# Sparse attention and mixture of experts: early pieces with the weights as fixed operand, and 232 rows for the last two ranks

## The chip, the core and the metric

The kernel runs on one core of a Trainium2 chip. A core has TensorE (PE, whose weight loads the profile lists apart as PEld), VectorE (DVE), ScalarE (ACT), GpSimd (POOL) and SyncE (SP), which work side by side and wait for each other on semaphores. The metric is the device time of one execution in microseconds (us). Before the change the median of three runs is 350.05 us (350.0 to 353.05).

## The reference, cut to what matters

```python
scores = scale * np.matmul(q, k.transpose(0, 1, 3, 2))      # 4 batches, 8 heads, 576 positions, 64 wide
scores = np.where(masks, scores, -1e9)                      # 4 heads: a window of 32; 4 heads: every 32nd position
attn = softmax(scores); x = (attn @ v) as 2304 tokens x 512
logits = x @ w_gate                                         # 8 experts
expert_idx = argmax(logits); gate_w = softmax(logits)[expert_idx]
h = maximum(x_of_expert @ w1[e], 0)                         # 512 -> 1024
y = h @ w2[e]                                               # 1024 -> 512
out[token] = gate_w * y                                     # all float32; an expert takes at most 576 tokens
```

With the inputs of the reference's seed the eight experts get 348, 339, 329, 279, 278, 271, 231 and 229 tokens.

## The kernel before, in words

**Attention and routing** come first. PE, DVE and ACT walk through an order written out by hand. As logits become known, the tokens get an expert and a place in its list (`r_top`, `r_pos`, `r_slot`, `r_tab`: short DVE chains with small matmuls between them, all in the PSUM tile `R_`).

**The expert that will be the fullest is known early**, from the first 1536 tokens. While the routing of the last tokens still runs, its first 128 tokens ("the pieces") go through the whole expert in plain float32. This is the generator `early` (L932 to L971). `up(c)`, for c of 0 to 3, makes 128 tokens x 256 features: the turned tokens `x` are the fixed operand (lhsT), the weights `loads[c][0]` the moving one, 256 columns wide, over four slices of the 512 inputs. ACT takes the maximum with 0 (L946, tile `hs`). Features then have to lie on partitions for the second layer, so `turn(c)` (L949) turns two 128 x 128 blocks on PE with the identity (L952), and ACT copies them to `ht` (L953). `down(f)` (L955), for f of 0 to 7, adds one slice of the second layer to `y0p`, 128 x 512; ACT copies the sum to `keep["y"]` (L971). `ep(k)` runs k steps of the generator, and L1035 to L1094 place these steps among the routing's last matmuls. In float32 each matmul instruction of the program shows as two matmuls and two weight loads in the profile, called passes below; a turn shows as one. `x_steps(1)` and `x_steps(2)` (L1067 to L1077, matmuls L1072) turn the next two gathered blocks of tokens of this expert, for the stage after.

**The expert stage** takes the experts by rank of their token count. How many rows each rank has is fixed by a tuple of `SETS`; the smallest set that holds all counts is chosen by a branch (L1447). Rank 0 has 352 - 128 = 224 rows left, since the pieces took 128. Numbers are split in two halves of type fp32r, so each product is three matmuls. `gemm1` (L1254) is 12 matmuls for each of 8 blocks of features, with the weights fixed and the tokens moving, n columns wide. Where n is at most 256 (`tm`: rank 0 and the last two ranks), the second layer is `gemm2_t` (L1277): 6 matmuls per block, whose moving operand is the weights, always 512 wide. The other ranks use `gemm2`, n wide. Weights stream in ahead of use.

**PSUM** has eight banks. Before the expert stage: `ps_t` three banks, `ps_s` one tile of two (banks 3 and 4), `ps_o` one tile of two (5 and 6), `R_` one. `h0` and `y0p` are both tiles of `ps_s`, `h1` is of `ps_o`. In the expert stage `ps_y` has the banks 0 to 3, `ps_h` the banks 4 and 5 (the first `ph` is in bank 4), `ps_x` the banks 6 and 7. A tile of the new stage waits for the last reader of the old tile in the same bank.

Of the kernel before, what the change touches and what calls it, by code (L numbers as in the profile page):

```python
# [9 lines left out]
F32 = mybir.dt.float32  # L10
# [4 lines left out]
AF = mybir.ActivationFunctionType  # L15
# [17 lines left out]
WARM = 9  # L33
SPLIT = (3, 4, 5)
SETS = (
# [3 lines left out]
)  # L39
# [12 lines left out]
def kernel(  # L52
# [10 lines left out]
    nc = tc.nc  # L63
# [6 lines left out]
    KD = DM // 128  # L70
# [28 lines left out]
    ident = const.tile([128, 128], F32, name="ident")  # L99
# [51 lines left out]
    with ExitStack() as p1:  # L151
# [5 lines left out]
        wk = p1.enter_context(tc.tile_pool(name="wk", bufs=3))  # L157
        tmp = p1.enter_context(tc.tile_pool(name="tmp", bufs=2))
        ps_t = p1.enter_context(tc.tile_pool(name="ps_t", bufs=3, space=PSUM))
        ps_s = p1.enter_context(tc.tile_pool(name="ps_s", bufs=1, space=PSUM))  # L160
# [753 lines left out]
        regs, loads, g0 = {}, {}, {}  # L914
# [17 lines left out]
        def early(x):  # L932

            h = [ps_s.tile([128, 2, 512], F32, tag="s", name="h0"), None]
            hs = wk.tile([128, 4, 2, 128], F32, tag="x", name="hs0", bufs=2)
            ht = wk.tile([128, 8, 128], F32, tag="x", name="ht0", bufs=2)
            y = None

            def up(c):
                if c == 1:  # L940
                    h[1] = ps_o.tile([128, 2, 512], F32, tag="o", name="h1")
                o = h[c % 2][:, c // 2, 0:256]
                for d in range(KD):
                    nc.tensor.matmul(o, lhsT=x[:, d], rhs=loads[c][0][:, d], start=d == 0, stop=d == KD - 1)
                    if d == KD - 1:
                        nc.scalar.activation(hs[:, c].rearrange("p a f -> p (a f)"), o, AF.Relu)  # L946
                    yield

            def turn(c):  # L949
                t = ps_t.tile([128, 2, 128], F32, tag="t", name="th0")  # L950
                for a in range(2):
                    nc.tensor.transpose(t[:, a], hs[:, c, a], ident)  # L952
                nc.scalar.copy(ht[:, 2 * c:2 * c + 2], t)  # L953

            def down(f):  # L955
                nc.tensor.matmul(y, lhsT=ht[:, f], rhs=loads[f // 2][1][:, f % 2], start=f == 0, stop=f == NF - 1)
                yield

            for c in range(4):
                u = up(c)  # L960
                next(u)
                yield
                if c:
                    turn(c - 1)
                yield from u
            y = ps_s.tile([128, 2, 512], F32, tag="s", name="y0p")[:, 0]
            for f in range(NF):
                if f == 1:
                    turn(3)
                yield from down(f)  # L970
            nc.scalar.copy(keep["y"], y)  # L971

# [4 lines left out]
        for i in range(-1, n):  # L977
# [11 lines left out]
            if i == n - 1:  # L989
                work0 = early(early_x())  # L990
# [491 lines left out]
```

## Time and profile before

| | us |
|---|---|
| median of three runs | 350.05 |
| the profiled execution | 347.72 |
| its span, first to last instruction | 346.0 |
| attention and routing, up to the first matmul of the pieces | 0 to 104.6 |
| pieces, beside the routing's last tokens | 104.6 to 124.3 |
| eight experts on PE | 125.0 to 340.7 |
| last scaling, last scatter to memory | 340.7 to 346.0 |

A profile lists for each engine when it was busy and what ended its idle time. An idle time matters only on an engine that others wait for, or that is itself never free later.

### The profile page before, as it was taken

What the parts mean: (1) busy time and instruction counts of PE and PEld (TensorE: products, weight loads), DVE (VectorE), ACT (ScalarE), POOL (GpSimd) and SP (SyncE); (2) the same over time, 40 slices, a digit from 0 to 9 for tenths busy, and PEclk for the clock granted to TensorE, in tenths of its full rate; (3) what the DMA queues carried; (4) which work ended last, traced back from release to release, by engine and by line L of the source; (5) the groups of instructions that cost most, each with busy time, mean ns of one, the idle gap of its engine ahead of it and who ended that gap; (6) DMA issues with size and microseconds to landing.
All of it is one profiled execution on the core that took longest, in us unless ns stands there. A gap on an engine that the chain in (4) does not pass through costs nothing. (4 is left out here: it accounts for less than half of the span.)

```text
span 346.0 us, 9916 instructions
## 1 busy us (share of the span) xinstructions
PE 333.6 (96%) x4023; PEld 295.6 (85%) x4024; DVE 213.3 (62%) x480; ACT 181.8 (53%) x342; POOL 119.9 (35%) x154
## 2 busy tenths in 40 slices
PE   8998999999999999999999999999999999999993
PEld 4777778777677568899999999999999999989992
DVE  7546466778975846654556555765765666665650
ACT  7686868767453344654434345354444454455531
POOL 8459456435010233065321450252251151121402
PEclk9999999999999999999999999999999999999998
DMA  6998998626099258078545554765575565665201
GB/s 207 310 216 269 277 185 241 150 73 132 20 311 350 61 181 265 19 214 276 191 136 159 176 184 122 234 219 176 170 252 145 193 224 189 192 231 147 101 1 64
DMA packets 51796, 62.85 MB, mean 182 GB/s; under 512 B 13622, under 2 KB 37192, under 8 KB 51741
## 3 DMA queue, kind: packets, MB, share of 16 engines
q1 hardware_dynamic: 47773, 52.20, 51.5%
q0 software_dynamic: 3968, 9.93, 8.3%
q8 instruction: 33, 0.54, 0.7%
q14 instruction: 22, 0.18, 0.2%
HBM read 52.67 MB, written 9.60 MB: 180 GB/s over the span
## 5 line engine op out<-in xcount | busy, mean ns | idle before, releaser
L1250 PE MATMUL ph<-xh,w1h 128*128 128x280 f32 (+5 forms) x252 | 76.8, 305 | 0.0
L1252 PE MATMUL ph<-xh,w1l 128*128 128x280 f32 (+5 forms) x252 | 74.0, 294 | 0.0
L1251 PE MATMUL ph<-xl,w1h 128*128 128x280 f32 (+5 forms) x252 | 74.0, 294 | 0.0
L1267 ACT ACTIVATE hh<-ph 128x280 fp32r<-128x280 f32 (+5 forms) x64 | 25.9, 405 | 89.3 <-PE ph L1252 87.1
L1295 POOL DMA_INDIRECT out_dram<-yo,routing x22 | 21.8, 992 | 122.2 <-DVE yo L1328 83.1
L1268 DVE SCALAR_TENSOR_TENSOR hl<-ph,hh 128x280 fp32r<-128x280 f32 (+5 forms) x64 | 28.8, 450 | 54.0 <-ACT hh L1267 54.0
L1250 PE MATMUL y<-hh,w2h 128*128 128x280 f32 (+3 forms) x160 | 48.2, 301 | 0.0
L1250 PEld LDWEIGHTS ph<-xh,w1h 128*128 128x128 f32 x252 | 47.6, 189 | 0.7
L1251 PE MATMUL y<-hl,w2h 128*128 128x280 f32 (+3 forms) x160 | 48.2, 301 | 0.0
L1252 PE MATMUL y<-hh,w2l 128*128 128x280 f32 (+3 forms) x160 | 48.2, 301 | 0.0
L1251 PEld LDWEIGHTS ph<-xl,w1h 128*128 128x128 f32 x252 | 47.7, 189 | 0.5
L1252 PEld LDWEIGHTS ph<-xh,w1l 128*128 128x128 f32 x252 | 47.6, 189 | 0.0
L1230 DVE TENSOR_TENSOR w1l<-w1r,w1h 128x1024 fp32r<-128x1024 f32 x31 | 38.0, 1226 | 15.0 <-ACT w1h L1229 13.9
L1230 DVE TENSOR_TENSOR w2l<-w2r,w2h 128x1024 fp32r<-128x1024 f32 x31 | 38.0, 1225 | 11.6 <-ACT w2h L1229 11.1
L1229 ACT CAST w2h<-w2r 128x1024 fp32r<-128x1024 f32 x31 | 32.2, 1040 | 0.0
L1229 ACT CAST w1h<-w1r 128x1024 fp32r<-128x1024 f32 x31 | 32.2, 1040 | 0.0
L1252 PEld LDWEIGHTS y<-hh,w2l 128*128 128x128 f32 x160 | 30.1, 188 | 0.0
L1250 PEld LDWEIGHTS y<-hh,w2h 128*128 128x128 f32 x160 | 30.1, 188 | 0.0
L1251 PEld LDWEIGHTS y<-hl,w2h 128*128 128x128 f32 x160 | 30.1, 188 | 0.0
L1340 POOL DMA_INDIRECT gt<-g_dram,routing x22 | 24.8, 1127 | 13.5 <-DMA xg<-x_dram,idx 7.1
L142 POOL DMA_INDIRECT xg<-x_dram,routing x19 | 19.3, 1014 | 24.0 <-PE px L1240 13.5
L224 POOL COPY v0l<-v0l 32x1088 f32<-32x1088 f32 x16 | 18.3, 1141 | 7.8 <-DMA v0l<-in_v_dram 6.9
(237 smaller groups left out, 629.8 us busy)
## 6 DMA issues: line engine op xcount, KB each, us to landing
w1r<-in_moe_w_dram SPq DMA_DIRECT2D x32, 512.0 KB
w2r<-in_moe_w_dram SPq DMA_DIRECT2D x32, 512.0 KB
vz<-in_v_dram SPq DMA_DIRECT2D x16, 144.0 KB
lk<-in_k_dram SPq DMA_DIRECT2D x4, 576.0 KB
lq<-in_q_dram SPq DMA_DIRECT2D x4, 576.0 KB
v0l<-in_v_dram SPq DMA_DIRECT2D x16, 144.0 KB
x_dram<-xz SPq DMA_DIRECT2D x16, 144.0 KB
x_dram<-xl SPq DMA_DIRECT2D x8, 256.0 KB
```

Of the source, the lines that this page charges most:

```text
L142: nc.gpsimd.indirect_dma_start(out=t[:r], out_offset=None, in_=x_dram[0:rows, :], in_offset=bass.IndirectOffsetOnAxis(ap=idx[:r], axis=0),)
L224: nc.gpsimd.tensor_copy(vt[64 * h:64 * h + 32, 1:18, h, 0:64], vt[64 * h + 32:64 * h + 64, 0:17, h, 0:64])
L1229: nc.scalar.copy(hi, t)
L1230: nc.vector.tensor_tensor(lo, t, hi.bitcast(F32), op=ALU.subtract)
L1250: nc.tensor.matmul(o, lhsT=wh, rhs=xh, start=first, stop=False)
L1251: nc.tensor.matmul(o, lhsT=wh, rhs=xl, start=False, stop=False)
L1252: nc.tensor.matmul(o, lhsT=wl, rhs=xh, start=False, stop=last)
L1267: nc.scalar.activation(hh, o, AF.Relu)
L1268: nc.vector.scalar_tensor_tensor(hl, o, 0.0, hh.bitcast(F32), op0=ALU.max, op1=ALU.subtract)
L1295: s = nc.gpsimd.indirect_dma_start(out=out[:, :], out_offset=bass.IndirectOffsetOnAxis(ap=idx, axis=0), in_=o, in_offset=None, bounds_chec ...
L1340: nc.gpsimd.indirect_dma_start(out=t[:r], out_offset=None, in_=g_dram[:, :], in_offset=bass.IndirectOffsetOnAxis(ap=idx_r(i)(j)[:r], axis=0),)
```

## The change

Three things change. In `up(c)` the weights become the fixed operand and the 128 turned tokens the moving one: the result lies with its features on partitions, ACT writes the maximum with 0 straight into `ht`, and `turn`, `hs` and ACT's copies go. Each of the 16 matmuls of 256 columns becomes two of 128; the generator yields as often as before. `y0p` moves from the two banks of `ps_s` to one bank of `ps_t`. The last two ranks of the smallest set get 232 rows instead of 256. Lines behind this place stand 9 lower in the new program (L1261 is L1252 there, L1447 is L1438).

```diff
-    (352, 344, 336, 280, 280, 272, 256, 256),
+    (352, 344, 336, 280, 280, 272, 232, 232),
...
-            hs = wk.tile([128, 4, 2, 128], F32, tag="x", name="hs0", bufs=2)
             ht = wk.tile([128, 8, 128], F32, tag="x", name="ht0", bufs=2)
...
                 o = h[c % 2][:, c // 2, 0:256]
-                for d in range(KD):
-                    nc.tensor.matmul(o, lhsT=x[:, d], rhs=loads[c][0][:, d], start=d == 0, stop=d == KD - 1)
-                    if d == KD - 1:
-                        nc.scalar.activation(hs[:, c].rearrange("p a f -> p (a f)"), o, AF.Relu)
-                    yield
-
-            def turn(c):
-                t = ps_t.tile([128, 2, 128], F32, tag="t", name="th0")
                 for a in range(2):
-                    nc.tensor.transpose(t[:, a], hs[:, c, a], ident)
-                nc.scalar.copy(ht[:, 2 * c:2 * c + 2], t)
+                    for d in range(KD):
+                        nc.tensor.matmul(
+                            o[:, 128 * a:128 * a + 128], lhsT=loads[c][0][:, d, 128 * a:128 * a + 128], rhs=x[:, d],
+                            start=d == 0, stop=d == KD - 1,
+                        )
+                        if a and d == KD - 1:
+                            nc.scalar.activation(ht[:, 2 * c:2 * c + 2].rearrange("p a f -> p (a f)"), o, AF.Relu)
+                        if d % 2:
+                            yield
...
             for c in range(4):
-                u = up(c)
-                next(u)
-                yield
-                if c:
-                    turn(c - 1)
-                yield from u
-            y = ps_s.tile([128, 2, 512], F32, tag="s", name="y0p")[:, 0]
+                yield from up(c)
+            y = ps_t.tile([128, 512], F32, tag="t", name="y0p")
             for f in range(NF):
-                if f == 1:
-                    turn(3)
                 yield from down(f)
             nc.scalar.copy(keep["y"], y)
```

On PE, between the tables of the tokens before last (`R_` at L672) and the positions of the last ones (L628), the second and third `up` and one turn (`th`) stood among the routing; h are the sums of `up`:

```order
-L944 MATMUL h_2558<-w1r,x_2462 128x256 x2
-L944 MATMUL h_2511<-w1r,x_2462 128x256
-L952 MATMUL th_2610<-ident,hs_2512 128x128 x2
-L944 MATMUL h_2511<-w1r,x_2462 128x256
+L944 MATMUL h_2561<-x_2462,w1r 128x128 x4
+L944 MATMUL h_2511<-x_2462,w1r 128x128 x4
 L628 LDWEIGHTS tri
 L628 MATMUL R__129<-oh,tri 128x16
```

Four matmuls of 256 columns and two turns became eight matmuls of 128 columns, ahead of the same L628.

On ACT, from the first sum of the pieces to their last:

```order
-L946 ACTIVATE hs_2512<-h_2511 128x256
-L1041 CAST w1h<-w1r 128x1024
-L545 COPY xtl<-txl 128x512
-L953 COPY ht_2513<-th_2560 128x256
-L946 ACTIVATE hs_2512<-h_2558 128x256
-L953 COPY ht_2513<-th_2610 128x256
+L949 ACTIVATE ht_2512<-h_2511 128x256
+L1032 CAST w1h<-w1r 128x1024
+L545 COPY xtl<-txl 128x512
+L949 ACTIVATE ht_2512<-h_2561 128x256
```

The copies of the turned blocks are gone; the cast of the first expert's weights (`w1h`) and the copy `xtl` stay behind the first maximum.

On PE at the start of the expert stage, with the engines whose semaphores are waited for; before:

```order
L956 MATMUL y0p<-w2r,ht_2513 128x512 [waits DMAHW4_49,Activation_49]
L956 MATMUL y0p<-w2r,ht_2513 128x512
L1447 COMPARE_AND_BRANCH
L1261 MATMUL ph<-xh,w1h 128x224 [waits Activation_49]
L1261 MATMUL ph<-xh,w1h 128x224 x3
```

and now:

```order
L954 MATMUL y0p<-w2r,ht_2512 128x512 [waits DMAHW4_49,Activation_49]
L954 MATMUL y0p<-w2r,ht_2512 128x512
L1438 COMPARE_AND_BRANCH
L1252 MATMUL ph<-xh,w1h 128x224 [waits PE_49,Activation_49]
L1252 MATMUL ph<-xh,w1h 128x224 x3
```

Before, the first `ph` waited for ACT's copy of `y0p` (L971). Now it waits for ACT's cast of the last turned tokens, the instruction ahead of that copy, and for PE matmuls of `up`, long ahead.

## Rows read from the trace of the kernel before

**Rows 1.** The page: busy time, and the clock granted to TensorE in 40 slices.

```profile
PE 333.6 (96%) x4023; PEld 295.6 (85%) x4024; DVE 213.3 (62%) x480; ACT 181.8 (53%) x342; POOL 119.9 (35%) x154
...
PEclk9999999999999999999999999999999999999998
```

**Rows 2.** All waits of PE from 104 us on: total us, times, longest.

```profile
PE ph L1261 <- ACT y L971: 0.8, 1, 0.8
PE LPl L576 <- ACT xtl L545: 0.4, 1, 0.4
PE R__129 L672 <- DVE r_pe L637: 0.3, 1, 0.3
```

**Rows 3.** Timeline of PE, pieces' stage: start, duration, line, tiles [idle before].

```profile
107.88 0.38 PE L952 MATMUL th<-ident,hs 128*128 128x128 f32 x2
...
109.07 0.31 PE L576 MATMUL LPl<-wg,xtl 128*32 128x8 f32 x16 [0.36 <-ACT xtl L545]
...
109.91 1.54 PE L944 MATMUL h<-w1r,x 128*128 128x256 f32 x6
...
112.21 0.17 PE L628 MATMUL R__129<-oh,tri 128*128 128x16 bf16 x1
...
112.79 1.54 PE L944 MATMUL h<-w1r,x 128*128 128x256 f32 x6
...
115.08 0.26 PE L672 MATMUL R__129<-r_rh,r_ol 128*128 128x40 bf16 x4
115.19 1.11 PE L944 MATMUL h<-w1r,x 128*128 128x256 f32 x4
116.13 1.02 PE L956 MATMUL y0p<-w2r,ht 128*128 128x512 f32 x2
116.99 0.38 PE L952 MATMUL th<-ident,hs 128*128 128x128 f32 x2
117.21 1.88 PE L956 MATMUL y0p<-w2r,ht 128*128 128x512 f32 x4
...
121.52 2.74 PE L956 MATMUL y0p<-w2r,ht 128*128 128x512 f32 x6
125.03 0.68 PE L1261 MATMUL ph<-xh,w1h 128*128 128x224 f32 x4 [0.77 <-ACT y L971]
```

**Rows 4.** Timeline of ACT, the same stage.

```profile
108.43 0.59 ACT L545 COPY xtl<-txl 128x512 f32<-128x512 f32 x1
...
124.30 0.59 ACT L971 COPY y<-y0p 128x512 f32<-128x512 f32 x1 [1.99 <-PE y0p L956]
```

**Rows 5.** Timeline of DVE: the last tokens' table operands.

```profile
114.03 0.32 DVE L657 TENSOR_TENSOR r_rh<-r_oa,vali 128x160 bf16<-128x160 bf16 x1
```

**Rows 6.** Timeline of POOL: the second gather of tokens ahead of the experts.

```profile
116.03 1.13 POOL L142 DMA_INDIRECT xg<-x_dram,idx  x1 [1.38 <-DVE t L730]
```

**Rows 7.** DMA issues from 100 to 130 us: these gathers, median us to landing.

```profile
xg<-x_dram,idx POOLq DMA_INDIRECT x2, 3.5
```

**Rows 8.** PE timeline: 12 first-layer matmuls, rank 0 (224 columns), then rank 7 (256).

```profile
132.01 0.27 PE L1250 MATMUL ph<-xh,w1h 128*128 128x224 f32 x1
...
133.34 0.40 PE L1282 MATMUL y<-w2h,hh 128*128 128x512 f32 x1
...
327.86 0.28 PE L1250 MATMUL ph<-xh,w1h 128*128 128x256 f32 x1
...
329.28 0.39 PE L1282 MATMUL y<-w2h,hh 128*128 128x512 f32 x1
```

**Rows 9.** Groups by line and shape: busy us, mean ns of one.

```profile
L1250 PE MATMUL ph<-xh,w1h 128*128 128x256 f32 x64 | 18.5, 289 | 0.0
...
L1250 PE MATMUL ph<-xh,w1h 128*128 128x344 f32 x32 | 10.5, 328 | 0.0
...
L944 PEld LDWEIGHTS h<-w1r,x 128*128 128x128 f32 x32 | 5.3, 190 | 0.3
```

**Rows 10.** Instructions of the branch on PE's queue: shortest, median, longest ns; first and last start.

```profile
L1447 PEldq COMPARE_BRANCH  x2: 90/1810/3529, 120.1 to 336.5; - x2
```

**Rows 11.** Timeline of the weight loads at the start of the experts.

```profile
125.00 0.52 PEld L1261 LDWEIGHTS ph<-xh,w1h 128*128 128x128 f32 x4 [1.56 <-issue]
```

**Rows 12.** Timeline of POOL: the last scatter.

```profile
341.71 1.02 POOL L1295 DMA_INDIRECT out_dram<-yo,routing  x1 [1.77 <-POOLq L1447]
```

## The prediction, made before the run

> **What bounds the kernel now.** I read the page first: PE is busy 96% of the span, and its clock is granted in full throughout [rows 1], so a change counts where it shortens PE's own chain. Busy shares are averages, so the next view is the list of everything that PE waited for after 104 us: three waits, 1.5 us in all [rows 2]. From the first expert matmul at 125.03 us to the end of its work PE waits for nothing: whatever PE saves there, and any earlier start of that stage, comes off the end. Then the timeline of PE in the pieces' stage [rows 3], where each start is read against the one before.
>
> **The weights as fixed operand.** A pass of 256 columns costs 0.215 us: six of them last 1.54 us and four 1.11 [rows 3], 0.43 for two more. A pass of 512 costs 0.43 (2.74 less 1.88 for two more). So 128 columns stream in about 0.107 us, and the 32 passes become 64 with the same columns in all. What is new is a weight load per 128 columns. The trace has no float32 pass of 128 columns with fresh weights. The nearest row is the first layer of rank 0: each matmul of 224 columns brings its own 128 x 128 load, and 12 take 133.34 - 132.01 = 1.33 us, 0.111 each [rows 8]. The load is of the same kind there (the pieces' own is listed with 190 ns [rows 9]; the cadence shows that most of this lies under the matmul before). Bounds for the pass: 0.107, the columns alone, and 0.218, columns and load one after the other (0.107 + 0.111). I take 0.111, because the row at 0.111 has the same load and nearly as many nanoseconds of columns.
>
> Now along PE. The first 16 passes end where eight did, within 0.05 us. The turn at 107.88 goes for nothing: PE then waits for ACT's `xtl` until 109.07, and this copy stands on ACT behind the first maximum and the weight cast, which do not move [rows 3, 4]. From 109.91: before, six passes, a turn and two passes reach L628 at 112.21, 2.30 us. After, 16 passes need 16 x 0.111 = 1.78, plus 0.08 for the first pass of a run, whose load nothing hides (four passes from 115.19 take 0.94 until 116.13, not 0.86 [rows 3]): 1.86. **Gain 0.44.** That turn cost twice its own time because PE waited for ACT in front of it. The next run is alike, from 112.79 to L672 at 115.08: 2.29 becomes 1.86, gain 0.43, in all 0.87. L672 also needs DVE's operands, ready at 114.35 before [rows 5] and, as their chain hangs on L628, 0.44 earlier now, at 113.91; PE arrives at 114.21, so PE is still the later one, by 0.3 us. Four passes (0.94) become eight (0.97), gain 0.84. The turn at 116.99 goes: 117.21 - 116.99 = 0.22, in all **1.06 us**. What could be late next is the gather for the second turned block: issued at 116.03, landed 3.5 us later at 119.5 [rows 6, 7]. Its index comes from the table that L672 closes, so it moves 0.87 earlier, to 118.7, and PE wants it at about 120. No wait.
>
> ACT loses four copies, which nobody on the path waited for; `hs` frees SBUF only: nothing.
>
> **The sums in one bank.** `y0p` ends its six passes at 121.52 + 6 x 0.43 = 124.10, its copy on ACT runs from 124.30 to 124.89 [rows 4], and the first expert matmul, whose bank was that of `y0p`, starts at 125.03: 0.93 us in which PE issues nothing. Now this matmul waits for ACT's cast of the last turned tokens, which in the new times is done about 2 us before. So it can follow the last pass at once, at 124.10 - 1.06 = 123.04: **gain 1.99 us with the above**. The banks that `y0p` takes now belong to the second layer, first written over 2 us later, when the copy is done. Hidden under the old wait is the branch: PE's queue held its compare up to 3.53 us, from 120.1 to 123.6 [rows 10], then the first new weight load came at 125.00 [rows 11], just after the copy. How much of the 1.4 us between is the branch's own cannot be seen; ends are 0 and all of it. I take 0: the compare ends just as the last pass issues, and that pass lasts 0.43 us, cover for a restart of that size. If this cover is too short it is a rival below.
>
> **232 rows.** Twelve matmuls of 256 columns take 329.28 - 327.86 = 1.42 us, 0.118 each, against 0.111 for 224 [rows 8]. At 224 the weight load sets the pace, not the columns (0.093 at the full clock); 232 columns with the 0.012 that 256 show above their columns come to 0.108, still below the load. So 0.111, and 2 ranks x 96 x 0.0075 = **1.44 us**. Bounds: 1.1 if the pace is read off a straight line between 224 and 256, 1.9 if columns alone counted (24 columns, 10 ns each, 192 times). The second layer moves 512 columns per matmul whatever the rows: nothing. ACT's and DVE's tiles shrink by a tenth, off the path. The last scatter takes 1.02 us for 128 rows [rows 12], is on the path, and has 104 now: 0 to 0.2, I take 0.1.
>
> Here a rule of the Trainium skill differs: TensorE: Matmul & The Clock Gate, section Back-to-back issue gap, gives the isolated gap as columns / 2.4 plus 2.5 ns, so by this estimate 109 ns for 256 and 99 for 232. By it the two ranks would save 1.9 us and the whole change 4.0. The trace has 118 and, for 224 columns, 111 [rows 8]; it decides.
>
> **Sum.** 1.99 + 1.44 + 0.1 = 3.5 us. The profiled execution of 347.72 us would take 344.2. The runs' median is 350.05, 2.3 above the profiled one; the same saving from it gives **346.5 us**.
>
> **The rivals.**
> *The weight loads do not hide* (ends slower). If a float32 pass cannot run beside the load of the next, it costs 0.218 instead of 0.111. The 16 passes ahead of the first maximum delay ACT's cast and `xtl`, and so L576, by 16 x 0.107 = 1.7 us; 40 passes after it add 4.3. Together 6.0 us against the forecast: 352.5, 0.7% slower than before. It decides from a pass of about 0.17 us on, where 56 passes eat the 3.5. Against it: the cadence of 0.111 in rank 0 [rows 8], less than load and columns in sequence could give. For it: no row has just this form, and the float32 load is listed with 190 ns [rows 9]. Chance 6%.
> In the same page of the Trainium skill, section The mechanism says that a weight load overlaps running matmuls only where it goes to another row group; all loads here use every row. By that rule this rival would be the forecast; the trace contradicts it at 224 columns.
> *The branch takes the place of the wait.* If all of the 1.4 us after the compare is the branch's own, the expert stage starts at 125.03 - 1.06 = 123.97, the gain is 2.6 and the time 347.5. For it: nothing is seen between 123.6 and 125.00 [rows 11]. Against it: the wait for the copy explains that gap alone, to 0.1 us. Chance 14%.
> *The narrow ranks give nothing*: another limit in the last two ranks (weights arriving, ACT, DVE) takes over. The time is 350.05 - 2.1 = 348. Against it: rank 0 runs at 224 columns with the same work beside it and PE waits for nobody [rows 2]. Chance 6%.
> *The smallest set no longer holds.* The tokens of the last ranks are 231 and 229 by the reference, one below 232. A single token decided otherwise sends the kernel to the second set. Columns of ranks 0 to 7 change by +32, +12, -4, +32, +18, +16, +18 and 0; 88 columns more cost 39 ns [rows 9], 0.44 ns each, times 192 matmuls (96 in rank 0): some 8 us, and rank 6 pays another 2 for its second layer by columns. 350.05 + 10 - 2 = 358. Against it: 279 and 271 tokens already stood one below their rows. Chance 2%.
>
> **The numbers.** That leaves 72% for the forecast, whose unknowns (a pass at 0.107 to 0.115, 232 columns at 1.1 to 1.9, the scatter) span about 1 us to either side with the spread of the runs: 345.5 to 347.6. The range takes in the branch and the narrow ranks without gain: 345.4 to 348.4. A measurement of this kernel tells about 1%, 3.5 us, from no change, and the forecast lies on that bound. Faster by over 1% (below 346.55): somewhat more than half of the forecast's cases and few others, 0.46. Within 1%: the rest of it, the branch, the narrow ranks, most of the loads that do not hide, 0.49. Slower by over 1%: the second set and the worst of the loads, 0.05.
>
> **What would show it.** Right: passes of `up` 0.111 us apart; L628 0.4 and the last L672 0.9 us earlier; no wait of PE for the copy of `y0p`, the first expert matmul near 123.0; 12 matmuls of 232 columns in 1.33 us; PE's last matmul 3.4 us earlier. Wrong: passes over 0.15 us apart, a gap of over half a microsecond in front of the first expert matmul with nothing to release it, 0.118 at 232 columns, or a new wait of PE for a gather, for weights or for DVE's tables.

## The result, and the profile after

The changed kernel takes 349.31 us in the median of 22 runs (345.1 to 357.49). The kernel before, run beside it on the same chip, takes 351.85 (22 runs, 346.78 to 358.21). The ratio is 0.9918, 95% interval [0.9889, 0.9948]: 2.9 us saved, between 1.8 and 3.9. All ratios here leave out the runs in the slower of the two states that executions of one program fall into, so they differ from the ratio of the medians of all runs, 0.9928 here. Two later comparisons of the same two kernels gave 0.994 [0.9894, 0.9986] and 0.9893 [0.985, 0.9936]. The forecast was 346.5, 3.5 below 350.05, with a range of 345.4 to 348.4. So the saving was nearly right, the time itself was not, and two things have to be explained: half a microsecond of the saving, and a level that lies above the three runs I had started from.

The profiled execution after takes 346.72 us, its span is 344.9, which is 1.1 less than before. The saving cannot be read off that difference either: the first matmul of the pieces starts at 106.51 us in it and at 104.59 before, behind 100 us of attention that the change does not touch. All that follows is therefore read from that first matmul on, which I call the start of the pieces.

The page, busy time and clock [rows 1], after:

```profile
PE 331.5 (96%) x4047; PEld 294.5 (85%) x4048; DVE 214.2 (62%) x480; ACT 179.8 (52%) x338; POOL 119.9 (35%) x154
...
PEclk9999999999999999999999999999999999999997
```

PE is busy 2.1 us less with 24 matmuls more. All waits of PE from 106 us on [rows 2]:

```profile
PE LPl L576 <- ACT xtl L545: 0.6, 1, 0.6
PE R__129 L672 <- DVE r_pe L637: 0.3, 1, 0.3
```

The wait for the copy of `y0p` is gone, and none has come in its place. The timeline of PE in the pieces, in the columns of [rows 3]:

```profile
106.51 0.69 PE L944 MATMUL h<-x,w1r 128*128 128x128 f32 x4
...
111.04 0.31 PE L576 MATMUL LPl<-wg,xtl 128*32 128x8 f32 x16 [0.56 <-ACT xtl L545]
...
111.88 2.03 PE L944 MATMUL h<-x,w1r 128*128 128x128 f32 x16
113.75 0.17 PE L628 MATMUL R__129<-oh,tri 128*128 128x16 bf16 x1
...
114.34 2.03 PE L944 MATMUL h<-x,w1r 128*128 128x128 f32 x16
116.20 0.26 PE L672 MATMUL R__129<-r_rh,r_ol 128*128 128x40 bf16 x4
...
122.45 2.74 PE L954 MATMUL y0p<-w2r,ht 128*128 128x512 f32 x6
124.63 1.00 PE L1252 MATMUL ph<-xh,w1h 128*128 128x224 f32 x4
```

Sixteen passes of 128 columns take 113.75 - 111.88 = 1.87 us, where 1.86 was forecast; the turn in front of L628 is gone. The last six passes of `y0p` run straight into the first expert matmul. The group of that matmul is listed 0.4 us early and long, because its first matmul stands behind the last pass; the row of its weight loads and the branch tell the true start:

```profile
124.60 0.19 PEld L1252 LDWEIGHTS ph<-xh,w1h 128*128 128x128 f32 x1 [0.24 <-issue]
125.03 0.41 PEld L1252 LDWEIGHTS ph<-xh,w1h 128*128 128x128 f32 x3 [0.24 <-issue]
```

```profile
L1438 PEldq COMPARE_BRANCH  x2: 90/1757/3424, 121.2 to 334.9; - x2
```

The compare stood in the queue from 121.2 to 124.6, and the first load of the experts follows at 124.60, on the same beat of 0.43 us as the loads of the passes ahead. The branch costs PE nothing.

In the last rank, timeline of PE [rows 8], 12 matmuls of 232 columns up to the second layer:

```profile
332.02 0.27 PE L1241 MATMUL ph<-xh,w1h 128*128 128x232 f32 x1
...
333.36 0.40 PE L1273 MATMUL y<-w2h,hh 128*128 128x512 f32 x1
```

1.34 us, 0.112 each, as forecast for 0.111. And the last scatter, timeline of POOL [rows 12]:

```profile
340.13 1.03 POOL L1286 DMA_INDIRECT out_dram<-yo,routing  x1 [1.78 <-POOLq L1438]
```

From its start to the end of the span are 344.9 - 340.13 = 4.77 us. Before they were 346.0 - 341.71 = 4.29. Here something was given back.

### The profile page after: what moved, and what is told of

Its sections match the earlier page's. It is cut to its first block, busy times and chain, and to the rows that moved or that the text cites. A ratio compares the mean times of both kernels' runs of the same rounds, so it can differ in the third digit from the quotient of the medians.

```text
span 344.9 us, 9962 instructions
## 1 busy us (share of the span) xinstructions
PE 331.5 (96%) x4047; PEld 294.5 (85%) x4048; DVE 214.2 (62%) x480; ACT 179.8 (52%) x338; POOL 119.9 (35%) x154
```

## The experiments

The table gives, for each profile, the times in us that the parts change. "First ph" is the recorded start of the experts (where no wait stands ahead of it, 0.4 us early, as above), "PE's end" the start of the last matmul, both counted from the start of the pieces; "tail" is from the start of the last scatter to the end of the span.

| kernel | start of pieces | first ph | PE's end | tail |
|---|---|---|---|---|
| before | 104.59 | 20.44 | 235.72 | 4.29 |
| after | 106.51 | 18.12 | 232.19 | 4.77 |
| 232 rows alone (s1) | 112.31 | 20.44 | 234.19 | 4.77 |
| fixed operand alone (s2) | 109.98 | 19.45 | 234.73 | 4.19 |
| one bank alone (s3) | 104.98 | 19.10 | 234.71 | 4.41 |
| after again (s4, a5) | 104.55, 107.81 | 18.12, 18.13 | 232.20, 232.20 | 4.72, 4.86 |
| cast behind `xtl` (e1, e2) | 110.16, 105.64 | 17.50, 17.49 | 231.88, 231.57 | 4.93, 4.76 |
| `v0l` spread (d1) | 110.89 | 18.13 | 232.48 | 4.80 |
| 248 and 240 rows (c1) | 110.35 | 18.12 | 232.98 | 4.37 |
| 64-column passes (h1) | 108.53 | 24.38 | 238.78 | 4.77 |
| 64 matmuls put ahead (f1) | 110.81 | 18.13 | 232.20 | 4.66 |
| more DMA packets (f2) | 108.36 | 18.12 | 232.20 | 4.81 |
| last rank 248 rows (t2) | 107.81 | 18.13 | 234.11 | 4.75 |
| last rank 240 rows (t1) | 111.52 | 18.12 | 233.72 | 4.56 |
| cast and 240 rows (t3) | 108.95 | 17.50 | 232.02 | 4.63 |

Executions of one program (after, s4, a5) agree within 0.01 us in the first ph and in PE's end, and lie 3.3 us apart in the start of the pieces; over all these kernels, which compute the same attention, that start goes from 104.55 to 112.31. (The experts lose up to 0.4 us at the start of the fifth rank in e1, d1, c1, h1, t1, t2 and t3, and 1.0 to 1.1 in the second rank in t1 and t2. The edit is not the cause: e1 and e2 are one kernel, and only e1 loses. What was late is not shown; the lists of waits name only one of 0.3 to 0.4 us for ACT's `hh`, in t1 and t2.)

### The three parts, one at a time

**232 rows alone**, on the kernel before:

```diff
-    (352, 344, 336, 280, 280, 272, 256, 256),
+    (352, 344, 336, 280, 280, 272, 232, 232),
```

> Only the 232 rows of the last two ranks, pieces as before. Theory A (every step is worth what the rows said, and the executions of any of these kernels differ by some us in the attention stage, which the change leaves alone): 12 matmuls of 232 columns take 1.33 us, the last two ranks' time on PE falls by 1.44 us, the ratio is 0.996. Theory B (part of the saving is given back by the change itself, by a later start of the pieces or a longer end): the last two ranks are 1.44 us shorter too, but the ratio is nearer to 0.998 to 1.000, since this edit is one of those that move the stages ahead or the last scatter.

Median 351.84, ratio 0.9955 [0.9896, 1.0014]. On PE 235.72 - 234.19 = 1.53 us, where 1.44 was forecast. The tail takes 0.48 of it back, so the "longer end" of Theory B is there.

**The fixed operand alone**, `y0p` still in `ps_s` and 256 rows:

```diff
-                    nc.tensor.matmul(o, lhsT=x[:, d], rhs=loads[c][0][:, d], start=d == 0, stop=d == KD - 1)
...
+                            o[:, 128 * a:128 * a + 128], lhsT=loads[c][0][:, d, 128 * a:128 * a + 128], rhs=x[:, d],
...
-                    turn(c - 1)
...
-                if f == 1:
-                    turn(3)
```

> Only the weights as fixed operand and the turns gone; y0p stays in the two banks of ps_s, 256 rows. Theory A: passes 0.111 us apart; from the first pass to L628 about 0.4 us less than before, to the last table matmuls (L672) 0.8, to the last pass of y0p 1.0; PE still waits some 0.8 us for the copy of y0p; saving 1.0 us, ratio 0.997. Theory B: the same inside the stage, but the first pass starts 1 to 2 us later than the 104.6 us of before, and the ratio is 1.000 or above.

On PE 235.72 - 234.73 = 0.99 us, forecast 1.06. The wait for the copy is still there, with its old size:

```profile
125.92 2.74 PE L954 MATMUL y0p<-w2r,ht 128*128 128x512 f32 x6
129.43 0.68 PE L1252 MATMUL ph<-xh,w1h 128*128 128x224 f32 x4 [0.77 <-ACT y L962]
```

The six runs say the reverse: median 353.61, ratio 1.0127 [1.0077, 1.0177]. More on this in the part on the level.

**One bank alone**, the last turn moved to `ps_s`:

```diff
-                t = ps_t.tile([128, 2, 128], F32, tag="t", name="th0")
+                t = (ps_s if c == 3 else ps_t).tile([128, 2, 128], F32, tag="s" if c == 3 else "t", name="th0")
...
-            y = ps_s.tile([128, 2, 512], F32, tag="s", name="y0p")[:, 0]
+            y = ps_t.tile([128, 512], F32, tag="t", name="y0p")
```

> Only y0p in one bank of ps_t (the last turn takes the two banks of ps_s instead, so that the third gathered block finds a free bank); turns and 256 rows stay. Theory A: PE does not wait for the copy of y0p, the first expert matmul follows the last pass within 0.1 us; saving 0.9 us, ratio 0.9975. Rival (the branch takes the place of the wait): a gap of 0.5 to 0.9 us stays in front of the first expert matmul, with no releaser, and the ratio is 0.999 to 1.000.

On PE 1.01 us, forecast 0.93; the first expert matmul follows the last pass without a gap, so the branch is free here too. Median 352.01, ratio 1.005 [1.0013, 1.0087].

**The whole change again**, beside these three:

> The whole change once more, on the same chip as its parts. Theory A: the parts add up, -1.4 -1.0 -0.9 = -3.4 us, ratio 0.990; the first pass of the pieces starts at another time than the 106.5 us of the first profile, by 1 us or more, since that is chance. Theory B: again at 106 to 107 us, later than in the three parts, and the ratio is 0.993 or above.

Median 348.5, ratio 0.994 [0.9894, 0.9986]; the pieces start at 104.55 us, so the later start in the first profile was not the change's. On PE 3.52 us. The parts, 1.53 + 0.99 + 1.01, make 3.53: they add up to a hundredth, and the forecast for PE was 3.43.

### How low the price of a pass goes

**Passes of 64 columns** (128 of them instead of 64):

```diff
-                            o[:, 128 * a:128 * a + 128], lhsT=loads[c][0][:, d, 128 * a:128 * a + 128], rhs=x[:, d],
+                                o[:, 128 * a + t0:128 * a + t0 + 64], lhsT=loads[c][0][:, d, 128 * a:128 * a + 128],
+                                rhs=x[:, d, t0:t0 + 64], start=d == 0, stop=d == KD - 1,
```

> The changed kernel with the pieces' 128 tokens moved in two halves of 64 columns: 128 passes instead of 64 in the first layer, each with its own weight load. Theory A (loads run beside matmuls, and a pass takes the longer of the two, 0.111 us for the load): passes stay 0.111 us apart though their columns are halved, so 32 passes take 3.55 us, and from the first pass to the first expert matmul it is about 5 us longer than the 18.5 us of the changed kernel. Rival (loads do not hide): 0.111 + 0.053 = 0.165 us a pass, 5.2 us for 32. If columns alone counted: 0.053 a pass and no change.

One run: 355.3 us. Timeline of PE:

```profile
115.81 3.76 PE L945 MATMUL h<-x,w1r 128*128 128x64 f32 x32
119.41 0.17 PE L628 MATMUL R__129<-oh,tri 128*128 128x16 bf16 x1
```

Thirty-two passes take 3.60 us, with 0.08 for the first load 0.110 each, against 0.112 with twice the columns. So half the columns save nothing. That this floor is the load's, and not that of any float32 pass, two lines of the changed kernel's profile show. At L594 four passes move 8 columns each, and their loads of 128 x 128 start at 107.53, 107.64, 107.76 and 107.87: 0.11 us apart. At L576 the loads are of 32 columns, and 64 passes of 8 columns take 0.65 us (111.04 to 111.69), 0.010 each. So the 0.111 that I had taken from rank 0 is the price of the load. The same L594 stands in the trace of before (its matmuls at 105.73, 105.84 and 105.95), and it is a row of the same float32 form, which the one I used is not. The pieces as a whole became 6.3 us longer (24.38 against 18.12), not the 5 that were expected: 64 more passes at 0.110 make 7.0, and the wait of 0.56 for `xtl` goes.

**248 and 240 rows** in the last two ranks of the changed kernel:

> The changed kernel with 248 rows for rank 6 and 240 for rank 7: the cadence of the first layer against its columns. Theory A (the weight load sets the pace below about 240 columns, the columns above): 12 matmuls of 248 columns take 1.38 us (0.115 each) and of 240 columns 1.34 to 1.35 (0.111 to 0.113). Rival (a straight line from 224 to 256): 0.1164 and 0.1146, 1.40 and 1.375 us.

One run: 350.86 us. Timeline of PE, one block of the last rank:

```profile
331.23 0.27 PE L1241 MATMUL ph<-xh,w1h 128*128 128x240 f32 x1
...
332.57 0.40 PE L1273 MATMUL y<-w2h,hh 128*128 128x512 f32 x1
```

Twelve matmuls of 240 columns take 1.34 us, as 12 of 232; 12 of 248 take 1.38 (the block at 317.52), 12 of 256 took 1.42 [rows 8]. Between 224 and 240 columns nothing is saved, above them about 0.04 us per 8 columns and block. The straight line (1.40 and 1.375) falls.

### The last scatter

The tail is 4.19 to 4.41 us in the four profiles with 128 rows in the last scatter or, in c1, 112, and 4.66 to 4.93 in the ten with 104 rows. **The last rank with 248 rows** (120 in the scatter) and **with 240** (112) were to tell why:

```diff
-    (352, 344, 336, 280, 280, 272, 232, 232),
+    (352, 344, 336, 280, 280, 272, 232, 248),
```

> The changed kernel with 248 rows for the last rank instead of 232, so that the last scatter has 120 rows. From its start to the end of the span the profiles had 4.19 to 4.41 us with 128 or 112 rows and 4.70 to 4.86 with 104. Theory T (the last scatter lands later when its rows are no multiple of 16; 104 and 120 are none): 4.7 to 4.9 us. Rival U (it is the number of rows as such, fewer rows landing later): between the two, 4.2 to 4.4 as with 112 and 128. On PE both expect 0.1148 instead of 0.111 per first-layer matmul of the last rank, 96 of them: 232.55 us from the first pass of the pieces to PE's last matmul instead of 232.2.

> The changed kernel with 240 rows for the last rank instead of 232. 12 matmuls of 240 columns took 1.33 to 1.34 us in c1, as 12 of 232 do, so PE's time from the first pass of the pieces to its last matmul stays at 232.2 to 232.3. The last scatter has 112 rows. Theory T and rival U: 4.3 to 4.4 us from its start to the end of the span, 0.4 less than the changed kernel. Rival V (the 0.45 us behind the last scatter do not come from its row count but from what else the 232 rows of the last two ranks change): 4.7 to 4.9 still. In the time 0.4 us below the changed kernel, 0.1%, at the edge of what the runs resolve.

Timeline of POOL, first t2 (span 348.1 us):

```profile
343.35 1.03 POOL L1286 DMA_INDIRECT out_dram<-yo,routing  x1 [1.78 <-POOLq L1438]
```

then t1 (span 351.2 us):

```profile
346.64 0.98 POOL L1286 DMA_INDIRECT out_dram<-yo,routing  x1 [1.75 <-POOLq L1438]
```

120 rows: 4.75 us, as with 104, so it is not that fewer rows land later. 112 rows: 4.56 in t1 and 4.63 in t3, after 4.37 in c1: between the others, and only in part below 104 rows. That 104 and 120 rows cost 0.2 to 0.7 us more than 128 is shown; that the multiple of 16 is the reason is in keeping with it but, with 112 in between, not shown. (PE's ends of t2 and t1, less the 1.5 us lost in the second and the fifth rank, are 232.6 and 232.2, as expected.)

The trace tells where the time goes. A scatter's semaphore gets sixteen marks as it lands. With 128 rows they come between 2.33 and 2.88 us after its start, with 104 rows three come at 2.0 us, the others from 2.85 on, and the last at 3.07 to 3.36; from the last mark to the end of the span it is 1.55 us in every profile. The packets of 4 KB that start 1.5 us or more behind the scatter's start took 0.16 to 0.17 us in the mean with 128 rows, 0.20 to 0.21 with 112 and 0.23 to 0.24 with 104 or 120. So the loss lies in the transfer, whose packets are slower; why they are stays open.

### What is still to be had

**The cast of the first expert's weights behind `xtl`** on ACT (`stage` holds the copy `xtl`):

```diff
+        stage("E", n - 1)
         nc.scalar.copy(W[0], ab[0])
-        stage("E", n - 1)
```

> The changed kernel with one line moved: ACT casts the first expert's weights (w1h) after its copy xtl, not ahead of it. In the profile after, PE waits 0.56 us at L576 for xtl, which starts 1 us late behind this cast. Theory: xtl and L576 come about 0.7 us earlier, everything on PE behind it too, and from the first pass of the pieces to the end of PE's work 231.5 us instead of 232.2; ratio to the kernel before 0.2% below that of the whole change (0.994 on the same chips). Rival: the routing's DVE chain, which hangs on L576 as PE does, is the later one and a wait of PE for DVE at L672 or L628 takes the place: gain under 0.2 us.

> The changed kernel with the cast of the first expert's weights behind the copy xtl on ACT, again, with five rounds. Theory K (the 0.6 us that L576 gains in the pieces reaches the end but for the 0.3 that the first profile lost in the sixth and seventh rank): 0.3 to 0.6 us below the changed kernel in the median, 0.1 to 0.2%, and 231.6 to 231.9 us from the first pass of the pieces to PE's last matmul. Rival L (the cast is now late for the first expert and takes it all back): no difference, 232.2. A difference of the medians above 1 us would be neither, but the spread of the attention.

> The changed kernel again, beside the next one on the same chip, to set the two against each other. Both theories: ratio to the kernel before 0.99 (0.985 to 0.995); from the first pass of the pieces to PE's last matmul 232.2 us.

L576 no longer waits for `xtl` and comes 0.62 us earlier; the first ph is 0.63 earlier (17.49 against 18.12), and in e2 PE's end is, too (231.57 against 232.20). In e1 0.3 of this was lost in the fifth rank. Medians: e1 350.05, ratio 0.9863 [0.9804, 0.9922]; e2 346.88, ratio 0.9864 [0.9798, 0.993], and beside it the changed kernel 348.49, 0.9893 [0.985, 0.9936]. The trace shows 0.6 us; the times lean the same way, but their intervals overlap, and the 1.6 us between the two medians are more than the trace can account for.

**Cast and 240 rows together:**

> The two edits that helped put together: the changed kernel with the cast behind xtl on ACT and 240 rows for the last rank. By the sum: 231.6 us from the first pass of the pieces to PE's last matmul, 4.3 to 4.4 from the last scatter to the end of the span; 1.0 us below the changed kernel, 4.1 below the kernel before from the first pass of the pieces on, a ratio of about 0.988. Rival: one of the two gains is lost to the other and it is 0.4 to 0.6 below the changed kernel.

Median 351.89, ratio 0.9907 [0.9873, 0.9941], beside t1 with 352.57, 0.9901 [0.9866, 0.9935]. First ph 17.50 and tail 4.63 as the parts have it; 0.4 us went in the fifth rank. The ratio expected was 0.988. That this version beats e2, or t1, is not shown.

### Where the level comes from

In the attention PE stops at places where the trace names nothing that it waits for. Timeline of PE, kernel s2:

```profile
50.02 0.33 PE L400 MATMUL oz<-v0s,ptz 36*64 36x65 f32 x4
52.37 1.09 PE L400 MATMUL oz<-v0s,ptz 36*36 36x65 f32 x28 [2.01 <-issue]
```

The stop lies inside a group of 32 equal matmuls. The same kernel by stretches of 4 us (length, then busy us and number of PE, PEld, DVE, ACT and POOL, PE's granted clock, DMA share, GB/s):

```profile
48.00:52.00 4.00, 2.35 (x44) 1.53 (x42) 1.92 (x3) 2.13 (x4) 2.40 (x3) 1.00 0.75 123
52.00:56.00 4.00, 3.63 (x74) 2.49 (x74) 1.06 (x3) 0.86 (x2) 3.83 (x4) 0.51 0.84 230
56.00:60.00 4.00, 4.00 (x61) 3.57 (x51) 2.60 (x9) 0.80 (x3) 2.49 (x3) 0.50 0.88 298
60.00:64.00 4.00, 4.00 (x85) 3.69 (x83) 0.46 (x3) 3.31 (x6) 0.92 (x2) 0.71 0.38 107
```

Behind the stop the granted clock is 0.5, that is 1.2 GHz, until 62.3 us. The pieces of s2 start 5.4 us later than those of s4, whose stops sum to 0.7 us and whose clock stays at 1.00. Such stops stand in every profile, and at the same places again and again: L365 near 17 us, L400 or L446 near 23, L472 near 30, L491 near 34, L400 near 52. I had put them down to the data first. They are not the only way to a low clock and a late start: in t1 and t3 PE waits 3.3 and 2.9 us, until 13.7 and 13.8 us, for ACT's `ps`, which hangs on DVE. The clock is then 0.5 for 6.8 us, and in t3, whose unnamed stops sum to 0.5 us, the pieces still start at 108.95.

**The loads of `v0l` spread** over the steps was to thin out the small packets at these places:

```diff
+                ready = [e for e in ready if e[1] != "lv" or i < 4 or (i % 2 and nput["lv"] == had)]
```

> The changed kernel with the loads of v0l (rows of 256 bytes) put into the load queue one batch at a time, at every second step, instead of two at once; the same loads. In all profiles with a late start of the pieces PE stops for 1 to 2.3 us around 50 us in the middle of 32 equal matmuls, with nothing that it waits for, while these loads and a fetch on the instruction queue run, and then its clock is granted at half. Theory C (the fetch of PE's instructions stands behind the burst of small packets): the stop goes or falls under 0.5 us, the mean granted clock of the runs rises from 0.990 to 0.995 or more and the median falls by 2 us or more, with the least time about the same. Rival D (the stop comes from something else, or the burst only moves): mean clock 0.988 to 0.992, median unchanged within 1 us, and the stop is found at another place.

Ratio 0.9869 [0.9822, 0.9915], median 349.01, but a stop of 2.2 us remained at L491, and the mean clock of the twelve runs is 0.989, as that of the 23 runs of the kernel before beside them: nothing was cured.

Counted in matmuls, stops of the same execution lie 126 (after), 377 (s4, e1, h1), 503 (s4) or 882 (s3) apart: 1, 3, 4 and 7 times about 126, each with as many weight loads. (Two places do not fit: L446 near 23 us lies 10 matmuls behind such a multiple, and a stop of 0.25 us at L400 near 13 us lies 79 ahead of the next place.) The page's DMA queues hold one called instruction, which up to 113 us moved, in s1:

```profile
q8 instruction: 18, 0.29, 1.2%
```

18 packets of 16 KB. So the suspicion: PE runs out of instructions at the ends of fixed pieces of its program.

**The program shifted by 64 matmuls**, which stand at its start:

```diff
-        warm(WARM)
+        t = ps_o.tile([128, 2, 512], F32, tag="o", name="warm")
+        for i in range(WARM + 64):
+            nc.tensor.matmul(t[:, i % 2, 0:64], lhsT=hot, rhs=hot[:, 0:64], start=True, stop=True)
```

> The changed kernel with 64 small matmuls more on PE ahead of the attention (73 warm-up matmuls of 64 columns instead of 9 of 512). The question is where PE stops in the attention with nothing that it waits for. In ten profiles such stops lie 126, 377, 502 or 878 matmuls apart, near multiples of 125.5, whatever stands there. Theory F (PE runs out of instructions at the ends of fixed pieces of its program, and the next piece comes late): the ends move 64 matmuls earlier in the program. No stop of over 0.2 us at L365 near 17 us, at L400 or L446 behind 341 matmuls, at the single tpl matmul of L491 near 34 us; stops instead, if any, within the group of 32 matmuls of L400 near 13 us, at L359 or L365 near 20, in L400 near 26, in L365 near 31, in L509 near 35 or 47, 0.3 to 2.3 us each. Rival G (something that these instructions need, data or a bank, is late and the profile does not name it): the stops stay at L365, L446, L491 and L400 as before, L491 above all.

One run, 350.81 us. Its stops over a microsecond, timeline of PE (lines stand 2 higher in number: L402 is L400, L511 is L509):

```profile
27.02 0.65 PE L402 MATMUL oz<-v0s,ptz 36*36 36x65 f32 x27 [1.43 <-issue]
...
52.86 0.64 PE L511 MATMUL ol<-v0l,ptl 128*32 128x130 f32 x14 [2.14 <-issue]
```

No stop remains at L365, at L491 or at L400 near 52. The new ones stand after 5 of the 32 matmuls of a group at L400 and after 18 of 32 at L509; a small one of 0.24 us, at 38.44, stands after 24 of 32 at L509. Counted from the program's first matmul, these three stand, in order of time, behind 472, 724 and 975 matmuls; in other profiles stops stand behind 472 (c1, t1, f2) and 974 (s1, s2, a5, e2), ahead of other work. So in this profile these stops go with the place in the program, not with the work; a fourth, of 0.25 us near 12 us, kept its work at L400 and is of another kind. That PE runs out of instructions at these places fits what was seen, but is not shown by itself.

**More packets on the DMA engines** were to show why the next piece is late:

```diff
+            if 4 <= i < 12:
+                nc.sync.dma_start(out=scr[i - 4], in_=v[i % 4, i // 4][:, 0:32])
```

> The changed kernel with eight copies more of 576 packets of 128 bytes each between two buffers in memory, one per step of the attention from the fifth to the twelfth; nobody reads what they write. Theory F, in its second half (the next piece of instructions is late because it stands behind other packets on the DMA engines): the sum of PE's stops without a releaser before the pieces grows from 0.7 to 2.6 us in the profiles so far to 4 us or more, at the same places as in the changed kernel, and the granted clock falls behind them. Rival H (the fetch is late for a reason of its own, whatever else moves): the sum stays within 0.7 to 2.6 us, and only waits for named transfers grow.

One run, 348.52 us: stops of 3.0 us in all, not 4 (c1 and h1 had 3.2 and 3.1 without these packets), and the clock of each of 40 slices at 9 tenths or more up to the last. The loads' queue filled 90% of the DMA engines' time between 18 and 62 us in s4 and fills 93% here, so little could be added; what makes a piece late stays open, and so does why some executions meet long stops and others short ones.

What the level is tied to, though, the runs show: of 92 runs of the kernel before that were taken beside the experiments, the 15 with a mean granted clock of at least 0.996 have a median of 349.9 us, the 26 at 0.986 or less one of 355.6. The means of s2's six runs and of the 29 runs beside them are 0.9862 and 0.9906, which goes the way of its ratio above 1, against the trace of the stage that s2 changes. So the ratios of s2 and s3 do not show their parts to be slower; at a level that moves by more than the parts, they can't price them. By the medians of all runs, 353.61 and 352.01 against 352.39, s2 is 0.3% above and s3 0.1% below the kernel before. An estimate at equal clock, from a straight line of time against mean granted clock through the 29 runs of the kernel before and those of one part (3.4 to 3.5 us for 0.01 of clock), puts s1 1.9 us below the kernel before, s2 0.3, s3 1.6 and the whole change (s4) 3.5, each to within 1.2 to 1.7 us. That agrees with the traces, though for s2 no saving at all lies within that bound too.

## Why the prediction was right and wrong

**What bounds the kernel**: right. What PE saved from the pieces on came off its end, if not all of it off the span (the last scatter, below), and the three parts add up to a hundredth of a microsecond.

**The weights as fixed operand**: right. A pass costs 0.112 us with the row of rank 0 as its price at 0.111; L628 comes 0.38 earlier (forecast 0.44), the last L672 0.80 (0.87), the last run of `y0p` 0.99 (1.06). The missing 0.06 lies in front of L576, where PE now waits 0.56 us instead of 0.36 for `xtl`. With passes at 0.112 the rival *the weight loads do not hide* falls: at 0.218 per pass 16 passes would have taken 3.5 us and not 1.87. The rule that a load overlaps only matmuls on another row group (the Trainium skill, TensorE: Matmul & The Clock Gate, The mechanism, which also names a background weight buffer as another way) does not agree with this trace: all these loads use every row, and in sequence with its load a pass of 64 columns would have been 0.053 us (half of 0.107) shorter than one of 128, where 0.002 were measured.

**The sums in one bank**: right, 1.01 us alone (0.93), and the branch is free; the rival that *the branch takes the place of the wait* falls with the load at 124.60.

**232 rows** on PE: right, 1.53 us against 1.44; the rival *narrow ranks give nothing* falls. The estimate by columns / 2.4 plus 2.5 ns (the Trainium skill, TensorE: Matmul & The Clock Gate, Back-to-back issue gap, which gives it for an isolated matmul and calls it too low for narrow ones, as it has no time for the load) gives 99 ns for 232 columns; measured are 112. The reason I gave was right as well: up to 240 columns the load sets the pace.

**The last scatter**: wrong in sign. I had taken "0 to 0.2, I take 0.1" off for 104 rows instead of 128; measured are 0.48 us more in the first profile after and 0.37 to 0.64 in the ten with 104 rows. That is the term of the sum that failed. 3.52 - 0.48 = 3.04 us are left of the profiles' saving, 0.9913 of 350, inside the intervals of all three ratios. I had read the price of a scatter as proportional to its rows, from POOL's 1.02 us; the time that follows that instruction, 3.27 us up to the end of the span, I had not looked at.

**Sum and numbers**: wrong on the level, and the range with it. The step that failed is the base of the forecast, "The runs' median is 350.05", from which the saving was taken off. With the 19 later runs beside the change added to those three, the median is 351.85, 1.8 us higher. With these 1.8 and the 0.5 us by which the saving fell short (3.04 instead of 3.53) 346.5 becomes 348.8, and the measured 349.31 lies half a microsecond above that sum, well inside the spread. The level alone brings the forecast to the upper end of the range (348.3 of 348.4), the scatter beyond it. The warning stood in front of me: 347.72, 350.0, 350.05 and 353.05 are four executions of one program, 5.3 us apart, and I had counted the spread as part of one microsecond. These four less the forecast saving of 3.53 span 344.2 to 349.5, which takes in the measured time. That a measurement could hardly tell 1% from nothing was right: the forecast on its bound came out at 0.8%.

## What to carry to other kernels

When a change makes a matmul narrower, find the floor first: the 4-byte 128 x 128 weight load set the pace here, in fp32r up to 240 columns and in float32 with 128 columns as with 64 or 8, and below such a floor fewer columns save nothing. Price the last transfer by the time to the end of the span, not by the instruction that issues it. And take the level of a forecast from the spread of all executions shown: here the attention, which the change leaves alone, ended anywhere within 7.8 us, over twice the whole change.

## What the runs showed of the hardware

- PE stopped up to 2.3 us at fixed places of its program, about 126 matmuls and as many weight loads apart; with 64 matmuls put ahead (f1, one profile) the stops kept their count and met other work. Behind some stops (2.01 us in s2, 2.19 in e1) the granted clock was 0.5 for 10.2 and 6.8 us; behind others (1.08 us in the changed kernel's profile) it stayed at 1.00.
- Float32 passes with a fresh 128 x 128 load took 0.112 us with 128 columns, 0.110 with 64 and 0.11 with 8.
- A last scatter of 104 or 120 rows took 0.2 to 0.7 us longer to the end of the span than one of 128, and its 4 KB packets 0.23 to 0.24 us in the mean against 0.16 to 0.17; 112 rows lay between.
